# Attention with inducing points and a squared-ReLU layer: the opening of batch 0, with three score groups of batch 1 made beside it

## The chip, the cores and the metric

The kernel runs on one core of one Trainium2 chip. The metric is the device time of one execution in microseconds, the median of several runs. Batches, token groups and weight chunks are counted from 0, as in the code: batch 1 is the second batch.

## The reference

```python
# x: 4 x 12480 x 128, inducing: 32 x 128, w_in: 128 x 2048, w_out: 2048 x 128
def mab(q, kv):
    s = scale * (q @ kv.transpose(0, 2, 1))
    s = s - s.max(-1, keepdims=True)
    a = np.exp(s)
    a /= a.sum(-1, keepdims=True) + 1e-09
    return a @ kv
h = mab(I, x)                 # 32 points per batch, from all 12480 tokens
y = mab(x, h)                 # every token attends to its batch's 32 points
r = np.maximum(y @ w_in, 0.0)
out = (s * (r * r) + b) @ w_out
```

The weights arrive as float64; the rest is float32.

## The kernel before, in words

**The order of the work.** Every engine runs its own queue in order. The kernel builds these queues with a planner (`class Plan`): each piece of work is a generator that yields the engine, a length in microseconds and the events it waits for; the planner keeps a clock per engine and always issues the piece that its clock and the urgencies (`SQ`, `OUT`, `FIRST`, ...) prefer. So a changed length or urgency anywhere can reorder everything behind it. Loads are issued on SyncE's queue (SP) in the order of the table `ORDER`, later of the list `loads`; eight DMA semaphores are used in turn, so that a load is issued only when the eighth one before it has landed.

**Batch 0, first pass.** The 12480 tokens of a batch are 26 blocks of 480, in 7 groups of four blocks (group 6 has two). For batch 0 the groups x0 to x6 come as 13 halves of 480 KB (`load_first`, L420). For each group `p1_unit` makes the scores of the 32 points (L480), a maximum, an exponential, the transposed exponentials (L500) and the value products (L511) over tokens that must lie turned (tokens on partitions). Eleven halves are turned on TensorE (`turn_x`, L453, eight transposes each); group 5 is in `TURNED`, and its two halves come a second time, already turned, from a DRAM copy `xQ` (`load_turned`, L441, 120 partitions of 4 KB). Meanwhile `narrow` makes float32 of the float64 weight chunks (four of w_in, four of w_out, 512 KB each, L316) in seven steps on VectorE and ScalarE (L331 to L348), and `split_w_out` scales w_out by `s` and splits it into two float32r parts (L356, L358).

**From the last values to the first pair.** `h_unit` and `h_out` (L592, L609) combine the groups into the 32 points hT. `w_first` multiplies hT with each chunk of w_in (L632; the copies to `wst` on ScalarE, the residue on VectorE, L637): the points stand in for the tokens in the first layer. `attend_first` does the softmax of block 0 against the points (L843 to L870), turns it (L875) and copies it to `a2t` on ScalarE. Products that no one needs (`warm`, L1231) keep TensorE busy in the gaps.

**The main part.** For each block there are 8 pairs: two products a2t x wst (L928), a ReLU on ScalarE or VectorE (L942, L944), the square, rounded to float32r on ScalarE (L1010), the residue of the square on VectorE and GpSimd (L965, L987), and out products (L1035): two chunks times three parts, 64 products of 480 columns per block with the first two. The first `NATIVE` = 8 pairs (block 0) use two plain float32 products each instead, with the unsplit w_out. Beside the blocks of batch b run the attention of the same batch (L799) and, for batch b+1, scores (L701) and values (L742); some of them share a turn of TensorE (`visit`), with the tables `SCORES_WITH` and `VALUES_WITH` saying which group goes with which attention.

```python
# before.py, L86 on: batch 0 carries all seven score groups of batch 1
SCORES_WITH = (((6,), (0, 1), (2, 3), (4, 5), (), ()), ...
VALUES_WITH = (((), (), (), (), (0,), (2, 3)), ...
VALUES_AT = (((1, 20),), (), ())
```

Of the kernel before, what the change touches and what calls it, by code (L numbers as in the profile page):

```python
# [19 lines left out]
P = 128  # L20
T = 120
NQ = 4
# [14 lines left out]
SLIP = 0.1744  # L37
WEIGHT = 0.0178
LEAN = {'ACT': -0.5309, 'DVE': 0.6608}
R_LEAN = {'DVE': -0.2301, 'ACT': -0.2128}  # L40


M_U = -5.8018
R_U = 4.5067
SQ = 1.1237
MM = 0.2134
S_U = -0.7565
C_U = -10.6897
OUT_HI = 3.9914
OUT = 0.2122  # L50
FRONT = -1.1612
FIRST = -200.0
SPREAD = 74.0965
FIRST_FRONT = 0.3289
SPLIT_U = 237.6882

NATIVE = 8
H_U = -10.6844
N_U = -24.7788
W_IN_U = -167.7494  # L60
W_OUT_U = 10.3457
W_URGENCY = 3.9038
W_STEP = 19.8754
# [7 lines left out]
RUN = 512  # L71
A_OFF = 19
# [18 lines left out]
VISIT_U = -14.4858  # L91
# [3 lines left out]
class Plan:  # L95
# [7 lines left out]
    def __init__(self):  # L103
        self.free, self.events, self.units, self.end, self.start = {}, {}, [], 0.0, 0.0
        self.eng, self.by = None, {}
# [4 lines left out]
    def _step(self, unit, urgency, ready, src):  # L110
        want = next(unit, None)
        if want is not None:
# [9 lines left out]
            waits = [w for w in waits if not isinstance(w, float) and w != "both"]  # L122
            self.units.append([unit, urgency + more, (ready, src), engs, waits, urgency, lean, None, both])
# [26 lines left out]
    def run(self):  # L150
        while self.units:
            able = {}
            for u in self.units:
# [10 lines left out]
                able.setdefault(eng, []).append((at + WEIGHT * urgency, at, engs[eng], u))  # L164
# [7 lines left out]
            at, _, u, self.eng = min(picks, key=lambda x: x[0])  # L172
            self.units.remove(u)
            self.start, self.end = at, at + u[3][self.eng]
# [7 lines left out]
def tile_attn_relu2(ctx: ExitStack, tc: tile.TileContext, xT, xH, xN, xQ, indT, w_in, w_out, s_rep, b_rep, outT):  # L182
# [13 lines left out]
    const = ctx.enter_context(tc.tile_pool(name="const", bufs=1))  # L196
    xt_pool = ctx.enter_context(tc.tile_pool(name="xt", bufs=XT))
# [13 lines left out]
    def copy(out, in_):  # L211

        if plan.eng == "ACT":
            nc.scalar.copy(out=out, in_=in_)  # L214
        else:
            nc.vector.tensor_copy(out=out, in_=in_)

# [22 lines left out]

# [1064 lines left out]
```

## Time and profile before

| what | us |
|---|---|
| median of 3 runs | 1551.55 (1551.47 to 1551.56) |
| the profiled execution, its own time | 1552.4 |
| its span, first to last instruction | 1550.6 |
| TensorE busy | 1542.8 |
| VectorE, ScalarE, GpSimd busy | 1469.9, 1482.0, 1471.1 |
| first pair's products (L928) start | 46.36 |
| last out product ends, about | 1547 |

Busy time counts overlapping instructions of an engine once. The windows view gives it by stretch, the chain of waits names what each step waited for, and the timeline lists the instructions of an engine by start time; a merged row's length reaches to the end of its last instruction, so that neighbouring TensorE rows overlap, and the distance of two starts tells what a row really took.

### The profile page before, as it was taken

What the parts mean: (1) busy time and instruction counts of PE and PEld (TensorE: products, weight loads), DVE (VectorE), ACT (ScalarE), POOL (GpSimd) and SP (SyncE); (2) the same over time, 40 slices, a digit from 0 to 9 for tenths busy, and PEclk for the clock granted to TensorE, in tenths of its full rate; (3) what the DMA queues carried; (4) which work ended last, traced back from release to release, by engine and by line L of the source; (5) the groups of instructions that cost most, each with busy time, mean ns of one, the idle gap of its engine ahead of it and who ended that gap; (6) DMA issues with size and microseconds to landing.
All of it is one profiled execution on the core that took longest, in us unless ns stands there. A gap on an engine that the chain in (4) does not pass through costs nothing.

```text
span 1550.6 us, 24505 instructions
## 1 busy us (share of the span) xinstructions
PE 1542.8 (99%) x8135; PEld 1294.9 (84%) x8135; DVE 1469.9 (95%) x1648; ACT 1482.0 (96%) x1750; POOL 1471.1 (95%) x665
## 2 busy tenths in 40 slices
PE   9999999999999999999999999999999999999999
PEld 6688888888888888888888888888888888888887
DVE  5999999999999999999999999999999999999998
ACT  7899999999999999999999999999999999999998
POOL 0299999999999999999999999999999999999998
PEclk9999999999999999999999999999999999999999
DMA  8212321332233123123232321321313112112100
GB/s 300 64 56 80 122 72 71 114 130 96 68 111 115 39 103 115 39 103 115 71 85 80 118 76 66 115 80 65 112 60 96 32 52 71 40 44 71 57 22 32
DMA packets 53482, 130.12 MB, mean 84 GB/s; under 512 B 11262, under 2 KB 37758, under 8 KB 53358
## 3 DMA queue, kind: packets, MB, share of 16 engines
q1 hardware_dynamic: 53358, 128.56, 25.2%
q8 instruction: 66, 1.08, 0.3%
q14 instruction: 58, 0.48, 0.1%
HBM read 74.50 MB, written 25.56 MB: 65 GB/s over the span
## 4 chain that ended last, share of the span: by engine, by line
PE 96%; DMA 2%; DVE 1%; POOL 0%; issue 0%; ACT 0%; SPq 0%; ACTq 0%; DVEq 0%; POOLq 0%
PE x L1035 68%; PE h L928 23%; PE x L799 2%; PE h L742 1%; PE h L701 1%; DMA g<-in_w_in_dram 1%; DMA xn<-in_xQ_dram 1%; DMA s_sb<-in_s_rep_dram 0%; DVE g L965 0%; POOL g L987 0%; PE h L651 0%; ACT xn L214 0%; PE x L742 0%; PE x L511 0%; SPq L420 0%
## 5 line engine op out<-in xcount | busy, mean ns | idle before, releaser
L987 POOL TENSOR_TENSOR g<-g,g 128x960 fp32r<-128x960 f32 x657 | 1469.8, 2296 | 73.6 <-DVE g L965 67.8
L1035 PE MATMUL x<-g,w_hi 128*128 128x480 f32 x3296 | 1063.6, 375 | 0.0
L1010 ACT ACTIVATE g<-r 128x960 fp32r<-128x960 f32 (+1 forms) x805 | 796.2, 1029 | 16.5 <-DVE r L944 2.4
L965 DVE SCALAR_TENSOR_TENSOR g<-h,r 128x960 f32<-128x960 f32 x657 | 739.4, 1146 | 22.4 <-ACT r L942 14.2
L1035 PEld LDWEIGHTS x<-g,w_hi 128*128 128x128 f32 x3296 | 614.8, 187 | 91.8 <-POOL g L987 3.3
L942 ACT ACTIVATE r<-h 128x960 f32<-128x960 f32 x660 | 622.8, 969 | 27.3 <-PE h L928 26.3
L1035 PE MATMUL x<-g,w_lo 128*128 128x480 f32 x1648 | 617.3, 375 | 0.0
L928 PE MATMUL h<-a2t,wst 128*128 128x480 f32 x1664 | 484.7, 378 | 0.7 <-DVE g L965 0.7
L928 PEld LDWEIGHTS h<-a2t,wst 128*128 128x128 f32 x1664 | 306.6, 187 | 65.4 <-DVE x L805 7.3
L1035 PEld LDWEIGHTS x<-g,w_lo 128*128 128x128 f32 x1648 | 308.9, 187 | 42.8
L944 DVE TENSOR_SCALAR r<-h 128x960 f32<-128x960 f32 x172 | 197.7, 1150 | 9.5 <-PE h L928 7.1
L987 DVE TENSOR_TENSOR g<-h,g 128x960 fp32r<-128x960 f32 x167 | 192.6, 1154 | 12.7 <-ACT g L1010 1.3
L965 DVE SCALAR_TENSOR_TENSOR h<-h,r 128x960 f32<-128x960 f32 x167 | 193.1, 1157 | 6.4 <-ACT r L942 5.7
L1044 ACT ACTIVATE ob<-x,bias 128x480 f32<-128x480 f32 x103 | 68.0, 660 | 4.1 <-PE x L1035 3.9
L799 PE MATMUL x<-xt,hT 128*32 128x480 f32 x208 | 28.3, 578 | 0.0
L805 DVE STREAM_TRANSPOSE x<-x 128x480 f32<-128x480 f32 (+1 forms) x28 | 19.3, 688 | 2.2 <-PE x L799 2.1
L742 PEld LDWEIGHTS h<-xn,eT 128*32 128x32 f32 (+1 forms) x570 | 17.0, 109 | 5.0 <-issue 4.8
L823 DVE STREAM_TRANSPOSE x<-x 128x480 f32<-128x480 f32 (+1 forms) x28 | 19.5, 696 | 0.9
L742 PE MATMUL h<-xn,eT 128*32 128x128 f32 (+1 forms) x570 | 19.6, 273 | 0.0
L821 DVE TENSOR_TENSOR x<-x,l 128x480 f32<-128x480 f32 (+1 forms) x28 | 18.5, 661 | 0.7
L701 PE MATMUL h<-xt,ind_sb 128*32 128x480 f32 x156 | 19.1, 566 | 0.0
L810 DVE TENSOR_TENSOR x<-x,mx 128x480 f32<-128x480 f32 (+1 forms) x28 | 18.4, 656 | 0.1
(147 smaller groups left out, 375.4 us busy)
## 6 DMA issues: line engine op xcount, KB each, us to landing
xt<-in_xT_dram SPq DMA_DIRECT2D x41, 960.0 KB, 5.5
out_dram<-ob SPq DMA_DIRECT2D x104, 240.0 KB, 2.0
a2t<-hl SPq DMA_DIRECT2D x412, 60.0 KB, 2.0
xn<-in_xN_dram SPq DMA_DIRECT2D x18, 512.0 KB, 6.1
xn<-in_xN_dram SPq DMA_DIRECT2D x18, 448.0 KB, 6.7
r<-in_xH_dram SPq DMA_DIRECT2D x7, 480.0 KB, 8.2
xt<-in_xT_dram SPq DMA_DIRECT2D x7, 480.0 KB, 5.4
wst<-hl SPq DMA_DIRECT2D x48, 64.0 KB, 2.0
```

What stands on the lines that cost most here:

```text
L701: nc.tensor.matmul(ps[M * q:M * (q + 1), 0:BLK], ind_sb, xt[:, q], start=True, stop=True)
L742: nc.tensor.matmul(ps[M * c:M * (c + 1), 0:P], eT[0:rows, n], xn_tiles[b, g, half][0][0:rows, n - half * TH], start=m < P // M, stop=m + P ...
L799: nc.tensor.matmul(ps[M * q:M * (q + 1), 0:BLK], hT[:, 0:M], xt[:, q], start=True, stop=True)
L823: nc.vector.transpose(out=s, in_=s)
L928: nc.tensor.matmul(h[:, u, 0:BLK], wst[:, c * P:(c + 1) * P], A, start=True, stop=True)
L942: nc.scalar.activation(out=r, in_=hv, func=AF.Relu)
L944: nc.vector.tensor_scalar(out=r, in0=hv, scalar1=0.0, scalar2=None, op0=ALU.max)
L965: nc.vector.scalar_tensor_tensor(out=g, in0=hv, scalar=0.0, in1=r, op0=ALU.max, op1=ALU.mult)
L987: eng.tensor_tensor(out=g2, in0=g, in1=hi.bitcast(F32), op=ALU.subtract)
L1010: nc.scalar.activation(out=q["g1_t"][:, sl, :], in_=q["r_t"][:, sl, :], func=AF.Square)
L1035: nc.tensor.matmul(o, w, g, start=first and n == 0, stop=left == 0 and n == len(ops) - 1)
L1044: nc.scalar.activation(out=ob, in_=o, func=AF.Identity, bias=bias, scale=1.0 if scaled else s_sb)
```

## The change

Two groups come turned from DRAM instead of one: group 6 is added to `TURNED` (its one half is loaded to a buffer that an `hl` tile fills later, group 5's to the second `wst` buffer). So ten halves are turned on TensorE and three halves come turned. The scores of groups 6, 4 and 5 of batch 1 (`GAP`) are spawned with the opening: their loads stand in `ORDER` as ("n", ...), and they are no longer in the visits of batch 0, where value group 1 now goes with a visit instead of by itself. The raw w_out chunks and their split parts have buffers of their own (pool `w2`), where each pair of split tiles takes the place of two raw chunks. Of `narrow`, one step always runs on ScalarE or GpSimd, and in the chunks of `POOLED` another goes to GpSimd. The loads of `s` and `b` move from behind x1 to the end of `ORDER`. The planner's lengths are replaced; it gets an urgency per piece (`URGENT`) and a cost for changing between tiled and whole products (`SWITCH`).

```diff
-TURNED = (5,)
-ORDER = (
-    ("x", 0), ("x", 1), ("w_out", 0), ("x", 2), ("w_out", 1), ("x", 3), ("w_in", 0), ("x", 4), ("w_in", 1),
-    ("w_in", 2), ("x", 5), ("x", 6), ("w_out", 2), ("q", 5), ("w_in", 3), ("w_out", 3),
-)
-WARM = 6
+TURNED = (5, 6)
+X_HOME = (4, 1, 3, 0, 3, 2, 1)
+GAP = (6, 4, 5)
+ORDER = (('x', 0), ('w_in', 1), ('x', 1), ('x', 2), ('w_out', 2), ('w_out', 1), ('w_in', 0), ('w_out', 3), ('x', 3), ('x', 4), ('x', 5), ('x', 6), ('n', 6), ('q', 5), ('w_in', 2), ('q', 6), ('w_in', 3), ('n', 4), ('n', 5), ('w_out', 0), ('s', 0))
+SWITCH = 0.14
+POOLED = (('w_in', 2), ('w_out', 0), ('w_out', 2))
+GAP_U = 107.5895
+WARM = 7
...
-SCORES_WITH = (((6,), (0, 1), (2, 3), (4, 5), (), ()), ((0, 1), (2, 3), (4, 5), (), (), ()), ((0, 1), (2, 3), (4, 5), (), (), ()))
+SCORES_WITH = (((), (0, 1), (2, 3), (), (), ()), ((0, 1), (2, 3), (4, 5), (), (), ()), ((0, 1), (2, 3), (4, 5), (), (), ()))
...
-TOP_AT = (17, 11, 11)
-VALUES_WITH = (((), (), (), (), (0,), (2, 3)), ((), (), (), (0,), (1,), (2, 3)), ((), (), (), (0,), (1,), (2, 3)))
-VALUES_AT = (((1, 20),), (), ())
+TOP_AT = (11, 11, 11)
+VALUES_WITH = (((), (), (), (0,), (1,), (2, 3)), ((), (), (), (0,), (1,), (2, 3)), ((), (), (), (0,), (1,), (2, 3)))
+VALUES_AT = ((), (), ())
...
-        yield "ACT", 0.48
-        nc.scalar.activation(out=dst, in_=m, func=AF.Copy, scale=2.0**-20, bias=1.0)
+        yield dict(ACT=0.525, Pool=0.68), {"ACT": M_LEAN}, 0.0
+        if plan.eng == "ACT":
+            nc.scalar.activation(out=dst, in_=m, func=AF.Copy, scale=2.0**-20, bias=1.0)
+        else:
+            nc.gpsimd.tensor_scalar(out=dst, in0=m, scalar1=2.0**-20, scalar2=1.0, op0=ALU.mult, op1=ALU.add)
+        if name in POOLED:
+            yield "ACT", 0.525
+            nc.scalar.activation(out=m.bitcast(F32), in_=lo, func=AF.Copy, scale=2.0**-52)
+            yield "Pool", 1.37
+            nc.gpsimd.tensor_tensor(out=dst, in0=m.bitcast(F32), in1=dst, op=ALU.add)
+        else:
+            yield "DVE", 0.6, "both"
+            nc.vector.scalar_tensor_tensor(out=dst, in0=lo, scalar=2.0**-52, in1=dst, op0=ALU.mult, op1=ALU.add)
...
-        yield "DVE", 0.6, "both"
-        nc.vector.tensor_tensor(out=dst, in0=dst, in1=e.bitcast(F32), op=ALU.mult)
+        yield dict(DVE=0.6, Pool=1.37), 0.0, "both"
+        either().tensor_tensor(out=dst, in0=dst, in1=e.bitcast(F32), op=ALU.mult)
...
-        yield "ACT", 0.54, ("w_out", c)
-        nc.scalar.activation(out=w_hi[:, sl, :], in_=raw[:, sl, :], func=AF.Copy, scale=s_sb)
+        yield "ACT", 0.615, "s", ("w_out", c), *[("raw used", n) for n in mine], ("w2", half - 1)
+        if half not in w2:
+            w2[half] = [w2_pool.tile([P, 2 * WC // P, P], F32R, name="w2") for _ in range(2)]
+            plan.set(("w2", half))
...
+        nc.scalar.activation(out=w_hi, in_=raw[:, sl, :], func=AF.Copy, scale=s_sb)
...
+            elif what == "s":
+                yield "SP", 0.9
+                nc.sync.dma_start(out=s_sb, in_=s_rep)
+                nc.sync.dma_start(out=b_sb, in_=b_rep)
+                plan.events["s"] = landing(1.0)
+            elif what == "n":
+                yield from load_xt((), 1, n, 1)
+                i = GAP.index(n)
+                plan.spawn(
+                    scores(1, n, (lambda: bank[1], lambda: hs[0][:, 0])[i % 2],
+                           ("p1", 0, NG - 1), *([("scores", 1, GAP[i - 2])] if i > 1 else [])),
+                    FIRST + GAP_U + i + urgent("n", n),
+                )
```

Three places where instructions move. Line numbers of the second fence of each are the changed kernel's.

TensorE, from the attention of block 0 to its first five pairs. Before (L843 attention of block 0, L632 points times a chunk of w_in, L1231 products that nothing needs, L875 the turn into a2t, L928 pairs, L799 the next attention):

```order
L843 MATMUL x_85<-hT,xt 120x32 x4
L632 MATMUL h<-w_in_sb,hT 128x512 x2
L1231 MATMUL h<-g_115 128x480 x3
L1231 MATMUL h<-g_115 128x320 x2
L632 MATMUL h<-w_in_sb,hT 128x512
L1231 MATMUL h<-g_115 128x320
L875 MATMUL x_85<-accb,hl 128x120 x4
L632 MATMUL h<-w_in_sb,hT 128x512
L1231 MATMUL h<-g_115 128x320
L928 MATMUL h<-a2t,wst 128x480 x4
L799 MATMUL x_86<-xt,hT 32x480 x4
L928 MATMUL h<-a2t,wst 128x480 x6
```

and now (L972, L756, L1370, L1004, L1057, L928 in the same meaning; L830 the scores of batch 1):

```order
L972 MATMUL x_88<-hT,r 120x32 x4
L830 MATMUL h<-xt,ind_sb 32x480 x4
L756 MATMUL h<-w_in_sb,hT 128x512 x2
L830 MATMUL x_89<-xt,ind_sb 32x480 x2
L1004 MATMUL x_88<-accb,hl 128x120 x4
L1370 MATMUL h<-g_90 128x480 x2
L1057 MATMUL h<-a2t,wst 128x480 x2
L756 MATMUL h<-w_in_sb,hT 128x512 x2
L830 MATMUL x_89<-xt,ind_sb 32x480 x4
L1057 MATMUL h<-a2t,wst 128x480 x2
L928 MATMUL x_89<-r,hT 32x480 x4
L1057 MATMUL h<-a2t,wst 128x480 x6
```

Two of the three score groups stand ahead of the first pair, one behind it, and two of the four w_in products have moved behind it as well; over the whole opening 14 unneeded products before the first pair have become 9.

SyncE's loads, from the last halves of x. Before:

```order
L316 DMA g_301<-in_w_in_dram 128x1024
L420 DMA r<-in_xH_dram 128x960 x3
L316 DMA g_373<-in_w_out_dram 128x1024
L441 DMA xn<-in_xQ_dram 120x1024 x2
L316 DMA g_432<-in_w_in_dram 128x1024
L316 DMA g_441<-in_w_out_dram 128x1024
L892 DMA a2t<-hl 32x480 x8
```

and now:

```order
L535 DMA xt<-in_xH_dram 128x960 x3
L363 DMA xt<-in_xT_dram 128x960
L555 DMA wst<-in_xQ_dram 120x1024 x2
L393 DMA g_395<-in_w_in_dram 128x1024
L555 DMA hl<-in_xQ_dram 120x1024
L393 DMA g_409<-in_w_in_dram 128x1024
L363 DMA xt<-in_xT_dram 128x1920 x2
L393 DMA w_457<-in_w_out_dram 128x1024
L1346 DMA s_sb<-in_s_rep_dram 128x1
L1347 DMA b_sb<-in_b_rep_dram 128x1
```

A third turned half and a half of batch 1 have come in ahead of the last values' data; behind them stand two groups of batch 1, the last w_out chunk (chunk 0) and the loads of `s` and `b`.

VectorE, the softmax of block 0. Before (L850 to L870 are its steps, L348 a weight step, L637 the residue of a w_in product):

```order
L850 TENSOR_REDUCE mx_589<-x_85 120x4
L852 TENSOR_TENSOR x_85<-x_85,mx_589 120x128
L348 TENSOR_TENSOR w_in_sb<-w_in_sb,g 128x512
L856 TENSOR_REDUCE x_85<-x_85 120x4
L858 TENSOR_SCALAR x_85<-x_85 120x4
L861 RECIPROCAL l_599<-x_85 120x4
L637 TENSOR_TENSOR wst<-h,wst 64x512
L863 TENSOR_TENSOR x_85<-x_85,l_599 120x128
L637 TENSOR_TENSOR wst<-h,wst 64x512
L870 TENSOR_TENSOR hl<-x_85,hl 120x8x32
```

and now (L979 to L999 the steps, L429 a weight step, L833 the eviction of a score group):

```order
L979 TENSOR_REDUCE mx_598<-x_88 120x4
L981 TENSOR_TENSOR x_88<-x_88,mx_598 120x128
L429 SCALAR_TENSOR_TENSOR g<-g_409,g 128x512
L985 TENSOR_REDUCE x_88<-x_88 120x4
L987 TENSOR_SCALAR x_88<-x_88 120x4
L990 RECIPROCAL l_608<-x_88 120x4
L992 TENSOR_TENSOR x_88<-x_88,l_608 120x128
L833 TENSOR_SCALAR s,mx<-h 128x480
L999 TENSOR_TENSOR hl<-x_88,hl 120x8x32
```

Both residues have left this stretch, and one eviction has come in.

## Rows read from the trace of the kernel before

**Rows 1.** The page: span, and busy time, share, instructions of each engine.

```profile
span 1550.6 us, 24505 instructions
...
PE 1542.8 (99%) x8135; PEld 1294.9 (84%) x8135; DVE 1469.9 (95%) x1648; ACT 1482.0 (96%) x1750; POOL 1471.1 (95%) x665
```

**Rows 2.** Windows: stretch, length, busy (instructions) of PE, PEld, DVE, ACT, POOL; clock; DMA.

```profile
46.30:67.00 20.70, 20.70 (x100) 11.41 (x99) 20.33 (x29) 19.22 (x25) 0.76 (x1) 1.00 0.30 87
67.00:433.00 366.00, 366.00 (x1935) 307.77 (x1934) 348.52 (x394) 352.90 (x414) 363.64 (x163) 1.00 0.27 88
433.00:809.20 376.20, 376.20 (x1990) 320.01 (x1989) 362.10 (x405) 362.23 (x426) 373.64 (x168) 1.00 0.27 89
```

**Rows 3.** Waits of TensorE from 67 to 1551 us: total, times, longest.

```profile
PE h L928 <- DVE g L965: 0.7, 2, 0.4
```

**Rows 4.** Chain of waits, 20 to 48 us: start, length, what.

```profile
27.29 7.88 DMA xn<-in_xQ_dram
...
35.21 1.74 PE x L511 x44
...
37.51 0.64 PE h L609 x14
...
39.65 0.60 DVE w_in_sb L341
40.25 0.60 DVE g L343
...
41.39 0.59 DVE w_in_sb L348
...
42.65 0.70 DVE wst L637
...
43.70 0.69 DVE wst L637
...
44.91 0.54 PE x L875 x4
```

**Rows 5.** Timeline of TensorE: start, length to the last end, instruction.

```profile
15.32 1.09 PE L453 MATMUL h<-ident,r 128*120 128x128 f32 x8
...
40.57 1.96 PE L632 MATMUL h<-w_in_sb,hT 128*128 128x512 f32 x4
...
46.36 1.06 PE L928 MATMUL h<-a2t,wst 128*128 128x480 f32 x4
```

**Rows 6.** Windows of the opening, columns as in rows 2.

```profile
2.00:10.00 8.00, 7.94 (x46) 5.07 (x45) 1.29 (x5) 2.64 (x6) 0.00 (x0) 1.00 0.80 268
12.00:26.00 14.00, 13.77 (x186) 8.67 (x182) 10.21 (x23) 12.45 (x25) 0.00 (x0) 1.00 1.03 415
27.50:35.00 7.50, 6.36 (x74) 3.58 (x71) 6.17 (x16) 7.15 (x18) 0.00 (x0) 1.00 0.94 250
```

**Rows 7.** Windows of the scores of line L701 alone.

```profile
433.00:809.20 376.20, 6.36 (x52) 1.79 (x52) 1.00 0.27 89
```

**Rows 8.** Chain of waits, whole span: native and split out products.

```profile
52.38 3.25 PE x L1035 x8
...
1540.70 6.41 PE x L1035 x30
```

**Rows 9.** The page's groups: attention, values and scores on TensorE.

```profile
L799 PE MATMUL x<-xt,hT 128*32 128x480 f32 x208 | 28.3, 578 | 0.0
...
L742 PE MATMUL h<-xn,eT 128*32 128x128 f32 (+1 forms) x570 | 19.6, 273 | 0.0
...
L701 PE MATMUL h<-xt,ind_sb 128*32 128x480 f32 x156 | 19.1, 566 | 0.0
```

**Rows 10.** Timeline of VectorE and ScalarE, 36 to 48 us.

```profile
36.22 0.43 DVE L331 TENSOR_SCALAR g<-g 128x512 int32<-128x512 int32 x1 [1.06 <-DMA g<-in_w_in_dram]
...
45.48 0.56 ACT L214 CAST a2t<-x 128x480 fp32r<-128x480 f32 x1 [0.33 <-DVE wst L341]
...
47.03 0.97 ACT L942 ACTIVATE r<-h 128x960 f32<-128x960 f32 x1
```

More of the change, by code (lines that the diff above doesn't have):

```diff
@@ new lines @@
+URGENT = {
+    ('x', 3): -234.92,
+    ('w_in', 1): 384.17,
+    ('w', 1): 32.13,
+    ('n', 4): -165.82,
+    ('w', 0): -64.56,
+    ('turn', 4, 0): 27.09,
+    ('turn', 2, 1): 149.29,
+    ('x', 1): 14.97,
+    ('v', 6): 132.81,
+    ('turn', 2, 0): 24.44,
+    ('x', 6): 23.68,
+    ('x', 4): 29.01,
+    ('v', 5): 30.4,
+    ('turn', 0, 0): -1.93,
+    ('turn', 4, 1): 107.18,
+    ('x', 0): 28.8,
+    ('w_in', 3): -107.28,
+    ('w_in', 2): -33.54,
+    ('w_out', 0): 54.0,
+    ('e', 2): -73.1,
+    ('a',): -91.2,
+    ('split', 0): -52.36,
+    ('n', 2): -145.64,
+    ('n', 1): -53.73,
+    ('v', 1): 116.75,
+    ('turn', 6, 1): -158.08,
+    ('n', 6): 31.77,
+    ('turn', 3, 1): -58.68,
+    ('w_out', 1): 2.74,
+    ('w_in', 0): 6.86,
+    ('e', 4): -22.03,
+    ('turn', 1, 0): -1.74,
+    ('split', 1): -56.02,
+    ('turn', 5, 0): -28.41,
+    ('turn', 1, 1): 7.37,
+    ('w_out', 2): -4.46,
+    ('h',): -28.6,
+    ('v', 3): 7.59,
+    ('e', 6): -15.74,
+    ('turn', 5, 1): -19.49,
+    ('n', 3): 5.58,
+    ('split', 3): -0.2,
+    ('x', 2): 0.98,
+    ('n', 5): 1.62,
+    ('n', 0): 40.51,
+    ('turn', 3, 0): 31.87,
+    ('w_out', 3): -50.52,
+    ('e', 3): 27.69,
+    ('w', 3): 59.87,
+    ('w', 2): -21.65,
+    ('e', 5): -27.4,
+    ('e', 1): -29.11,
+    ('v', 4): 3.57,
+    ('e', 0): 0.92,
+}
@@ L121, in _step @@
             more = sum(w for w in waits if isinstance(w, float))
-            waits = [w for w in waits if not isinstance(w, float) and w != "both"]
-            self.units.append([unit, urgency + more, (ready, src), engs, waits, urgency, lean, None, both])
+            kind = True if "tiled" in waits else False if "whole" in waits else None
+            waits = [w for w in waits if not isinstance(w, float) and w not in ("both", "tiled", "whole")]
+            self.units.append([unit, urgency + more, (ready, src), engs, waits, urgency, lean, None, both, kind])
     def extend(self, us):
@@ L392, in homes @@
     def homes():
+        for _ in range(XT):
+            ring("xt", XT)
         for _ in range(2):
-            ring("xt", XT)
             ring("r", 2)
@@ L433, in x_used @@
         n = home["x", g]
[L434 to L435 removed]
+        if g == left["x"][n][-1] and g:
+            plan.set(("xt", n) if n < XT else ("r", n - XT))
     def load_turned(g):
@@ L446, in turn_x @@
         j = g * GR // SB + h
-        yield "PE", 0.99, *waits, ("x half", j), ("v done", j - 4)
+        n = turns.index(j)
+        if j:
+            yield "PE", 0.88, "whole", *waits, ("x half", j), *([("v done", turns[n - 4])] if n > 3 else [])
+        else:
+            yield "PE", 0.44, "whole", *waits, ("x part", 0, 0)
         xt = xt_tiles[0, g, 1][0].rearrange("p q (s t) -> p q s t", t=T)
-        t = home["xn"][j % 4]
+        t = home["xn", j].rearrange("p (a q c) -> p a q c", a=SB, q=NQ)
         ps = ps()
         for a in range(SB):
+            if a and not j:
+                yield "PE", 0.44, "whole", ("x half", j)
             for q in range(NQ):
@@ L683, in scores @@
         rows = M * nb
-        if b not in st:
+        if b not in begun:
+            begun.add(b)
+            yield "DVE", 0.15, *waits
             d = st[b] = {
@@ L1034, in out_part @@
         for n, (w, g) in enumerate(ops):
-            nc.tensor.matmul(o, w, g, start=first and n == 0, stop=left == 0 and n == len(ops) - 1)
+            nc.tensor.matmul(o, w(), g, start=first and n == 0, stop=left == 0 and n == len(ops) - 1)
         used()
@@ L1051, in out_part @@
         plan.set(("ob", blk_g))
+    turned_0 = wst_pool.tile([P, F], F32, name="wst")
+    turns = [j for j in range(NSB) if j * SB // GR not in TURNED]
     w_out_raw = wst_pool.tile([P, NF, P], F32, name="wst")
@@ L1130, in chain @@
                 for want in f(*args, ps):
-                    yield (*want, ("ob", blk_g - 1) if blk_g else "first") if first else want
+                    start = [("ob", blk_g - 1)] if blk_g else ["first", *[("scores", 1, g) for g in GAP[0::2]]]
+                    yield (*want, *start) if first else want
                     first = False
@@ L1191, in turn_work @@
         yield from turn_x(g, h, lambda: hs[turns.index(j) % 2], ("turn", before[turns.index(j)]))
-    turns = [j for j in range(NSB) if j * SB // GR not in TURNED]
     before = [-2, -1, *turns]
```

232 lines of the change are left out of this document (134 added, 98 removed).

## The prediction

> **What bounds the kernel now.** First the page: TensorE is busy for 1542.8 of the 1550.6 us of the span [rows 1], so nothing can move the time but TensorE's own work and the few microseconds in which it idles. Then the windows, by batch: from 67 us on TensorE is busy in the whole of each stretch, at a granted clock of 1.00 [rows 2], and in the waits of that time it stands idle in sight for 0.7 us in all [rows 3]. Thirty split products take 6.41 us, 0.214 us each [rows 8], and come back to back to the end. So the main part costs what its products cost. What else there is to win lies ahead of the first pair, at 46.36 us [rows 5].
>
> There the chain of waits tells what ends last, and it is not TensorE. From 27.29 to 35.17 us the chain is one piece: the two turned loads of group 5 [rows 4]. The windows say why: the DMA engines move 415 GB/s from 12 to 26 us, and 250 from 27.5 to 35, while they are busy all the time [rows 6]. Only then come the last value products (35.21), the 32 points (h_out, 37.51), steps of VectorE, the turn into `a2t` (44.91) and the first pair [rows 4, 5]. Between h_out and that turn VectorE is the bound, and other work stands in the chain there: weight steps (0.60, 0.60, 0.59) and two residues of the points' layer (0.70, 0.69) [rows 4].
>
> **The change, part by part.** The profiled execution took 1552.4 us, its span 1550.6; the median of the runs is 0.85 below the first. I make the sum as a difference within the profile and add it to the median.
>
> *A. The last turned load lands later.* Two loads come in ahead of it: half a group of batch 1 (480 KB) and a third turned half. At 415 GB/s 480 KB take 1.18 us [rows 6]. A turned half is dearer: the 7.5 us window at 250 GB/s moved 1.88 MB, of which 0.98 MB were the two turned halves; the other 0.90 MB at 415 GB/s take 2.15 us, which leaves 5.35 us, 2.7 for each [rows 6]. The low bound is an ordinary half's 1.18, the high one half of the chain's row, 7.88 / 2 = 3.94 [rows 4]. I take 2.7, as it is worked out from the bytes moved. Something is won back: the loads of `s` and `b`, 128 rows of one number each, leave the start. The window from 2 to 10 us moved 268 GB/s [rows 6]; at 415 it would have moved (415 - 268) x 8 us = 1.18 MB more, 2.8 us of transfer. The trace does not tell how much of that is theirs and how much the start itself; between 0 and 2.8 I take 1.3, near the middle. So the landing is at 35.17 + 1.18 + 2.7 - 1.3 = 37.75 us, with bounds 35.17 + 1.18 + 1.18 - 2.8 = 34.7 and 35.17 + 1.18 + 3.94 = 40.3.
>
> The Trainium skill says in "DMA: Bandwidth & Descriptors", section "Why a DMA increments its semaphore by 16 and not by 1", that a transfer spreads over the largest number of engines up to 16 that divides its partitions. For 120 that is 15, and by that rule alone an estimate for a turned half is 16/15 of 1.18, 1.26 us; the sum would be 1.4 us lower, near 1550.9. The 250 GB/s of the row stand against it, so I keep to the row.
>
> *B. From the landing to h_out.* Before, the values after the landing take 1.74 us (44 records, half of them weight loads, so 22 products), and h_out starts 0.56 us after their end [rows 4]. Now the last load feeds 8 products: 8 / 22 x 1.74 = 0.63. So h_out starts at 37.75 + 0.04 + 0.63 + 0.56 = 38.98, which is **+1.47** against 37.51.
>
> *C. From h_out to the first pair.* Both residues leave VectorE's softmax stretch (0.70 + 0.69), one weight step goes out ahead of the maximum, of whose 0.60 some 0.4 stood in the way, as attend_first starts only at 39.65; an eviction of a score group comes in. Its nearest row is a residue of about its size, 0.69 [rows 4]. -0.70 - 0.69 - 0.4 + 0.69 = **-1.1**; bounds -1.6 (the eviction falls in a gap) and -0.3 (the steps moved out were hidden by the exponential). So the first pair starts at 46.36 + 1.47 - 1.1 = 46.7.
>
> *D. Work that now stands behind the first pair.* Two of the four w_in products of 512 columns, and score group 5, come after it, where TensorE is busy 20.70 of 20.70 us [rows 2] and so pays for all of it. Two such products take less than 1.96 us, a merged length that reaches over the next product's start, and 0.90 each by their pitch in the row [rows 5]: 1.8 with bounds 1.6 and 1.96. A score group is 8 records of the 52 that take 6.36 us in a batch [rows 7], 0.98. Together **+2.8**.
>
> *E. The main part loses three score groups.* They are 20 of these 52 records: 20 / 52 x 6.36 = **-2.45** us [rows 7], all of it on the packed engine.
>
> *F. What costs nothing.* One turn of a half (eight transposes, 15.32 us, 1.09 [rows 5]) goes; TensorE had no part in the chain while it waited for the turned loads, so that is worth 0 as long as the load lands last. The same holds for the two score groups ahead of the first pair: they take the place of products that nothing needs (1.51 us at 41.97 among others) [rows 4, 5]. The weight steps moved to ScalarE and GpSimd and the own homes of w_out make VectorE's queue shorter, away from the chain. ScalarE gets two scale copies of w_out straight behind the copy into `a2t` (45.48) and ahead of its first ReLU (47.03) [rows 10]; they wait for `s`, now the last load. Between the landing at 37.75 and `s` stand 2944 KB of other loads, 7.3 us at 415 GB/s [rows 6], so `s` lands after 45.1, about when the copy into `a2t` begins; ScalarE's first ReLU may move by a microsecond or two. TensorE has D's 2.8 us of work meanwhile, so I take 0. The rest of the new order: TensorE runs packed before, so 0, with 1.5 either way.
>
> The sum: +1.47 - 1.1 + 2.8 - 2.45 = **+0.7**, or **1552.3 us**. With the bounds of A and of the order taken together this case's own range is 1550.2 to 1554.4: no change that a measurement of this kernel could tell, for which I take 0.2%, some 3.1 us.
>
> **The rivals.** *R1, the opening ends with TensorE, not with the load.* If the turned halves run at an ordinary pace, and the start regains its 2.8 us, the landing is at 34.7. Then h_out comes when TensorE gets there: 37.51 less the 1.07 it now waits for the loads and less the turn's 1.02, 35.4, or -2.1. With C, D and E: -2.1 - 1.1 + 2.8 - 2.45 = -2.85, **1548.7**. For it speaks that the rate of 250 may belong to other traffic of those 7.5 us; against it, that the slow window begins just where the turned loads do.
>
> *R2, the new order takes out small gaps in the main part.* From 46.3 to 1546.9 are 1500.6 us; 6,624 split products at 6.41 / 30 are 1415.3, the native ones cost about 10 more, attention 28.3, values 19.6, scores 19.1 [rows 8, 9]. Some 8 us are left, of which the points' and layers' products of three batches take about half. With 3 of the remaining 4 gone: **1549.3**. Against it: only 0.7 us of waiting is to be seen [rows 3].
>
> *R3, slower: the loads behind each other.* If a turned half costs the chain's 3.94 us and nothing is won at the start, the landing is at 40.3, +2.55. Then every load behind it moves too: w_out chunk 0 ends the 2944 KB behind it, 7.3 us, at 47.6; its seven narrowing steps took from 36.22 to the 41.98 of the last in the chain for a w_in chunk, 5.8 us [rows 4, 10], and the first native out product needs it (52.38 [rows 8]). It and the scale copies that hold ScalarE's queue until `s` is there add about 0.5: **1555.5**. This decides from a landing after about 39.7. For it: the chain's own row; against it: the bytes that the windows count.
>
> That the change does not do what it says is in the forecast already: the score groups were to fill time of products that nothing needs, yet one of three groups and two w_in products fall behind the first pair, so 2.8 of work take the place of 2.45.
>
> **How the numbers follow.** Forecast 0.56, R1 0.16, R2 0.12, R3 0.16. Faster by over 0.2% is below 1548.45: half of R1 and of R2, and little of the forecast, 0.19. Slower by over 0.2% is above 1554.65: R3 and a little of the forecast, 0.17. Within: 0.64. The range takes in the centres of all three rivals, 1548.3 to 1555.6.
>
> **What would show it.** Right: the last turned load lands at about 37.8 us, TensorE waits for it, h_out at 39.0, first pair at 46.7; between the first and second pair two w_in products and 8 score records; 32 instead of 52 score records of batch 1 behind it; busy to the last product at clock 1.00. R1 would show no wait for a turned load; R3 a landing near 40, and idle time of TensorE between 46 and 60 us with w_out chunk 0 or `s` as the releaser; R2 an opening as long as forecast and a shorter batch 1 or 2. The forecast is wrong if the first pair starts before 45 or after 49, or if batches 1 to 3 change in length by more than 1.5 us.

## The result, and the profile after

The changed kernel takes **1566.79 us** (median of 4 runs, 1565.68 to 1568.77) against 1551.55 (4 runs): ratio 1.0098, interval 1.0086 to 1.0111. It is slower by 15.2 us, where the forecast was 1552.3 and the range ended at 1555.6. The runs of the kernel before lie within 0.2 us of each other, those of the changed one are 3 us apart; its longest, 1568.77, has a mean granted clock of 0.997, the other three 1.000. The profiled execution took 1565.85 us, 13.45 more than the profiled one of before.

The page's first rows, span and busy times, to be held against [rows 1]:

```profile
span 1564.1 us, 24449 instructions
...
PE 1550.7 (99%) x8123; PEld 1300.2 (83%) x8123; DVE 1478.4 (95%) x1651; ACT 1476.3 (94%) x1738; POOL 1475.0 (94%) x675
```

TensorE has 12 instructions fewer and is busy for 7.9 us more. Where the time lies is told by the windows of the changed kernel, in the columns of [rows 2] (its first pair starts at 47.19, its first block ends at about 72.8 us):

```profile
46.90:72.50 25.60, 24.05 (x110) 12.14 (x110) 23.10 (x35) 21.57 (x28) 2.31 (x3) 1.00 0.23 68
72.50:438.80 366.30, 365.67 (x1914) 309.36 (x1914) 350.76 (x390) 352.78 (x412) 360.62 (x162) 1.00 0.25 82
438.80:818.10 379.30, 379.30 (x1990) 321.02 (x1989) 365.77 (x407) 360.86 (x422) 372.91 (x168) 1.00 0.26 88
```

Two things stand out. The first is the opening. ScalarE's eviction of the first block, before and now:

```profile
66.88 0.75 ACT L1044 ACTIVATE ob<-x,bias,s_sb 128x480 f32<-128x480 f32 x1
```

```profile
72.80 0.74 ACT L1173 ACTIVATE ob<-x,bias,s_sb 128x480 f32<-128x480 f32 x1
```

It starts 5.9 us later: so much the opening lost, and TensorE is idle for 1.55 us of the first row's stretch, where it was busy throughout in [rows 2]. The second is the main part. Batch 1, whose tables were not changed, has the same 1990 TensorE instructions as in [rows 2], the same clock, TensorE busy throughout, and takes 379.30 us instead of 376.20. Waits explain none of it; this is every wait of TensorE from 67 us on (compare [rows 3]):

```profile
PE x L1164 <- DVE hl L959: 0.9, 2, 0.5
```

So the products themselves had become longer. The last entry of the chain of waits is a run of split out products, in the changed kernel 40 of them:

```profile
1551.72 8.68 PE x L1164 x40
```

8.68 / 40 is 0.217 us, against 0.214 in [rows 8]. The starts of the instructions in the trace say it sharper (the pitch is the distance of two neighbouring starts; products followed after 217 to 222 ns are called 219s from here on): from 90 us on, 1,706 of some 4,890 out products are 219s, and the rest are nearly all followed after 213 to 215 ns; in the kernel before 22 are. Those at 219 are mostly every second product of a pair of two, they come in stretches of up to 90 us, and then the pitch is the ordinary one for some time. 1,706 at some 5.2 ns are 8.9 us, and the others are half a nanosecond longer too. That is two thirds of the 13.45 us, and nothing in the prediction had to do with it.

### The profile page after: what moved, and what is told of

Read it like the earlier page. It is cut to its first block, busy times and chain, and to the rows that moved or that the text cites. A ratio compares the mean times of both kernels' runs of the same rounds, so it can differ in the third digit from the quotient of the medians.

```text
span 1564.1 us, 24449 instructions
## 1 busy us (share of the span) xinstructions
PE 1550.7 (99%) x8123; PEld 1300.2 (83%) x8123; DVE 1478.4 (95%) x1651; ACT 1476.3 (94%) x1738; POOL 1475.0 (94%) x675
## 4 chain that ended last, share of the span: by engine, by line
PE 94%; DVE 2%; ACT 2%; DMA 1%; issue 1%; SPq 0%; POOL 0%; DVEq 0%; ACTq 0%; POOLq 0%
PE x L1164 67%; PE h L1057 22%; PE x L928 2%; PE h L871 1%; PE h L830 1%; DVE g L1094 1%; DMA hl<-in_xQ_dram 1%; ACT g L1139 1%; ACT r L1071 0%; DMA g<-in_w_in_dram 0%; DVE h L1094 0%; PE x L633 0%; PE h L573 0%; DVE r L1073 0%; PE h L775 0%
## 5 line engine op out<-in xcount | busy, mean ns | idle before, releaser
L1164 PE MATMUL x<-g,w 128*128 128x480 f32 x4944 | 1190.8, 377 | 1.0 <-DVE hl L959 0.9
L1164 PEld LDWEIGHTS x<-g,w 128*128 128x128 f32 x4944 | 927.7, 188 | 140.5 <-DVE hl L959 1.9
L1057 PE MATMUL h<-a2t,wst 128*128 128x480 f32 x1664 | 486.6, 379 | 0.1
L1057 PEld LDWEIGHTS h<-a2t,wst 128*128 128x128 f32 x1664 | 309.1, 188 | 63.7 <-issue 7.6
L1073 DVE TENSOR_SCALAR r<-h 128x960 f32<-128x960 f32 x176 | 202.4, 1150 | 15.9 <-PE h L1057 13.4
L928 PE MATMUL x<-xt,hT 128*32 128x480 f32 x200 | 27.3, 578 | 0.0
L943 DVE TENSOR_REDUCE x<-x 128x15 f32<-128x480 f32 (+1 forms) x28 | 18.4, 657 | 1.4 <-ACT x L941 1.1
L937 DVE TENSOR_REDUCE mx<-x 128x15 f32<-128x480 f32 (+1 forms) x28 | 18.1, 645 | 0.4
```

The costliest lines, as they stand in the source:

```text
L928: nc.tensor.matmul(ps[M * q:M * (q + 1), 0:BLK], hT[:, 0:M], xt[:, q], start=True, stop=True)
L1057: nc.tensor.matmul(h[:, u, 0:BLK], wst[:, c * P:(c + 1) * P], A, start=True, stop=True)
L1073: nc.vector.tensor_scalar(out=r, in0=hv, scalar1=0.0, scalar2=None, op0=ALU.max)
L1164: nc.tensor.matmul(o, w(), g, start=first and n == 0, stop=left == 0 and n == len(ops) - 1)
```

## The experiments

**The address of the weights.** In the kernel before, the split weights of w_out begin at byte 9024 of a partition, which is 320 within 512. Their own pool puts them at 10240, a multiple of 512. One product's weights take 512 bytes of a partition, so all of them begin at the same place within 512. The moving rows of the out products (the squares and their residues) begin at 460 within 512 in both. In the changed kernel alone the place was put back; in the kernel before alone it was moved, to three places; the order of every engine stays, and of the other tiles only five small constants, which no out product reads, change their place.

```diff
# a_w9024: the tiles of the split weights ahead of five small constants, not behind them
+    const2 = ctx.enter_context(tc.tile_pool(name="const2", bufs=1))
-    bias = const.tile([P, 1], F32, name="bias")
+    bias = const2.tile([P, 1], F32, name="bias")
...
# b_w10240: the same move in the kernel before, the other way round (the five lines are taken out further down)
+    bias = const.tile([P, 1], F32, name="bias")
+    ident = const.tile([P, P], F32, name="ident")
+    ones = const.tile([P, M], F32, name="ones")
+    rebias = const.tile([P, 1], F32, name="rebias")
+    sel = const.tile([P, P], F32, name="sel")
     w_hi = const.tile([P, NF, P], F32R, name="w_hi")
     w_lo = const.tile([P, NF, P], F32R, name="w_lo")
```

> The changed kernel with nothing but an address changed: the split w_out tiles begin at byte 9024 of a partition, where they begin in the kernel before, instead of 10240. Theory A (the address of the weights makes the second of two out products take 219 ns instead of 213): the 219s go, 1752 of them from 90 us on in the profile at 5.5 ns, 9.6 us, so 1557 us, and the runs agree within 0.3 us. Theory B (it is the new order of the work, or that the weights lie in four tiles): it stays at 1566 to 1568 us with as many 219s.

> The kernel before with nothing but an address changed: w_hi and w_lo begin at byte 10240 instead of 9024, where the changed kernel has them; order and instructions as before. Theory A (address): second out products at 219 ns in stretches, 1558 to 1563 us, runs that differ by 1 us and more. Theory B (order or four tiles): 1551.5 us, no 219s.

> The kernel before with the split weights 64 bytes higher, at 9088: a multiple of 128 but not of 512. Theory A, if a multiple of 128 is what hurts: 1558 to 1563 us; if it takes a multiple of 512: 1551.5. Theory B: 1551.5.

> The kernel before with the split weights at 9216, a multiple of 512 (and 1024) as 10240 is. Theory A: 1558 to 1563 us, if the place within 512 bytes is what matters; 1551.5 if it is 10240 itself or a larger period. Theory B: 1551.5.

Measured: a_w9024 1558.63 us (ratio to before 1.0042, 1.0027 to 1.0056), b_w10240 1561.68 (1.0061, 1.0044 to 1.0078), b_w9088 1551.70 (0.9999, 0.9989 to 1.0010), b_w9216 1563.13 (1.0070, 1.0050 to 1.0090). The chain's last run of out products in b_w10240 and in a_w9024:

```profile
1549.65 6.51 PE x L1035 x30
```

```profile
1545.39 8.55 PE x L1165 x40
```

The reader is to hold 6.51 against the 6.41 of [rows 8] (the same 30 products), and 8.55 against 8.68 above (the same 40). Theory A holds in both directions: 8.2 us of the 15.2 go with the address (1566.79 to 1558.63), and the kernel before loses 10 to 11 us with nothing but that move. Neither the new order nor the four tiles are needed for it. What is left to explain is 6.9 us.

The 8.2 is less than the address cost the main part. From the first block's eviction to the last one's the profile of the changed kernel takes 1487.6 us and that of a_w9024 1478.0, so 9.6 us; but the opening of a_w9024's profiled execution is 3.2 us longer (its first block's eviction starts at 75.98). There the last turned load lands at 39.59 us, not 37.65, TensorE is busy for only 2.5 of the 6 us from 34 to 40, and then its granted clock falls to half, 1.2 GHz, while it is busy throughout (windows, columns as in [rows 2]):

```profile
38.00:40.00 2.00, 0.66 (x8) 0.60 (x10) 1.60 (x8) 1.82 (x6) 0.62 (x1) 0.99 1.02 392
40.00:42.00 2.00, 2.00 (x28) 1.97 (x24) 1.43 (x3) 0.59 (x3) 1.27 (x1) 0.50 1.02 420
```

From the last landing to the first pair it takes 10.74 us there and 9.54 in the changed kernel's profile, where the clock stays at 1.00. The profile of a_g19 (below), with its weights at 10240, has such a stretch at half clock too, so it does not come with the address.

A second set asked which of the two places counts. It moves the rows by 64 bytes, or puts the weights at 448:

```diff
-G_OFF = 3
+G_OFF = 19
```

> The changed kernel as it is, split weights at 10240, with only the squares (the moving operand of the out products) 64 bytes further in their tiles. Theory G (it is the distance of the moving rows from the weights within 512 bytes): from 52 bytes it becomes -12, and the share of 219s changes, to none or to more. Theory H (it is the weights' own place, a multiple of 512): the 219s stay, 1566 to 1568 us.

> The kernel before with the split weights at 9152, which is 448 within 512, 12 bytes ahead of the moving rows (460 within 512). Theory G (the distance decides): it is the same distance of 12 as in a_g19 and the 219s are as many as there, some 2900, 1566 us or more. Theory H (a multiple of 512 is what hurts): none, 1551.5.

> The kernel before with only the squares (the moving operand) 64 bytes further in their tiles, 12 instead of 460 within 512; the split weights stay at 9024, 320 within 512. Theory G (the rows' distance behind the weights decides, small ones are bad): it is 204 bytes now, none of the 219s, 1551.5 us. Theory J (the rows' place alone is bad at 12, as in a_g19): 219s, 1560 us and more.

Measured: a_g19 1575.04 us (ratio 1.0149, 1.0131 to 1.0168), b_w9152 1558.14 (1.0036, 1.0023 to 1.0049), b_g19 1561.15 (1.0065, 1.0042 to 1.0088). All nine kernels together, the places counted within 512 bytes, the 219s from 90 us on (the first two products of a pair, a2t x wst, called up here, are named where more than 60 of them have that pitch too):

```
kernel      weights  rows   out products at 219    time us
before        320    460          22               1551.55
a_w9024       320    460          26               1558.63
b_w9088       384    460          33               1551.70
b_w9152       448    460         869  (+371 up)    1558.14
changed         0    460        1706               1566.79
b_w10240        0    460        1882               1561.68
b_w9216         0    460        1931               1563.13
b_g19         320     12        1659  (+235 up)    1561.15
a_g19           0     12        2928               1575.04
```

Both places matter. Theory H (only a multiple of 512) falls with b_w9152 and b_g19, theory G (only the distance) with b_w9152, whose distance of 12 is that of a_g19 with a third of the 219s, and its form that small distances are bad with b_g19 as well, at a distance of 204; theory J (only the rows' place) with b_w10240. What rule joins the two is left open. The Trainium skill says in "SBUF — State Buffer", section "Who interferes with whom", that TensorE reads its moving operand and its weights through two independent ports, and that only the port pair of VectorE and GpSimd is contended for. By that alone one would have expected these moves to cost nothing; the runs of the kernel before show 6 to 11 us for four of the five moves, and the measurement decides.

**The opening, with the tables of the change.** On a_w9024, so that the 219s don't blur them, four parts of the change were undone by its own tables: a weight step back from GpSimd, one score group back to the main part, one turned group less, `s` and `b` early.

```diff
# a_pool_w0
-POOLED = (('w_in', 2), ('w_out', 0), ('w_out', 2))
+POOLED = (('w_in', 2), ('w_out', 2))
# a_gap2 (ORDER, SCORES_WITH and VALUES_WITH of batch 0 with it)
-GAP = (6, 4, 5)
+GAP = (6, 4)
# a_turned1 (and no ('q', 6) in ORDER)
-TURNED = (5, 6)
+TURNED = (5,)
# a_s_early
-ORDER = (('x', 0), ('w_in', 1), ('x', 1), ('x', 2), ...
+ORDER = (('x', 0), ('w_in', 1), ('x', 1), ('s', 0), ('x', 2), ...
```

> The changed kernel with the split weights at 9024, and the narrowing step of w_out chunk 0 that the change gave to GpSimd back on VectorE; TensorE's order up to the second pair stays. In the changed kernel VectorE's step that makes the low part of w_out took 1.74 us instead of 0.70 while GpSimd's 1.28 us step ran, an eviction stood behind it, and TensorE waited 1.2 us for that. Theory C (the two engines hinder each other): the step is back near 0.7 to 0.8 us, TensorE's wait goes, and the first native out product comes some 1 us nearer to the first pair: about 1557.5 us against 1558.6. Theory D (that step is long for another reason): it stays at 1.7 us and the time at 1558.6.

> The changed kernel with the split weights at 9024 and only two score groups in the opening; group 5 goes back into a visit of batch 0 (with the value groups of batch 0 as in the kernel before). Its 8 records leave the stretch between the first and second pair (0.98 us) and return in the main part (0.98 us). If the loss of the opening is TensorE's work and waits behind the first pair: from the first pair to the first native out product 8.2 us become 6 or less, and the whole is 1.2 us faster, 1557.4. If it is the late landing: no change of the whole, 1558.6.

> The changed kernel with the split weights at 9024 and group 6 turned on TensorE again, so that two turned halves are loaded instead of three. If the turned loads set the end of the opening, as the prediction has it: the last of them lands 2 to 3 us earlier, the 32 points and the first pair come 2 us earlier, the whole is 1556 to 1557 us. If the opening ends with something else by now: first pair at 47 us and later, 1558 to 1559.5, with the turn of one half more (1.1 us) on TensorE.

> The changed kernel with the split weights at 9024 and the loads of s and b back behind x1, as before the change. If they cost the start what the prediction took, 1.3 us of loading (bounds 0 and 2.8), the last turned load lands that much later and the whole is 1558.6 + 1.3 less what the scale copies gain from having s early. If they cost nothing there, it is 1558 us or a little less.

Measured: a_pool_w0 1571.55 us (ratio 1.0126, 1.0111 to 1.0141), a_gap2 1569.68 (1.0114, 1.0097 to 1.0131), a_turned1 1557.46 (1.0038, 1.0023 to 1.0053), a_s_early 1571.73 (1.0131, 1.0116 to 1.0146). Three of the four missed what every theory expected by 10 us or more. The planner had made another order of the whole kernel out of each edit. TensorE's longest waits from 67 us on in a_pool_w0:

```profile
PE h L1058 <- DVE g L1095: 3.6, 9, 0.8
PE x L1165 <- DVE hl L960: 1.2, 3, 0.5
PE x L1165 <- POOL g L1117: 0.9, 1, 0.9
PE x L1165 <- ACT g L1140: 0.3, 2, 0.2
```

a_w9024 waits there for 0.9 us in all. So the whole times of a_pool_w0, a_gap2 and a_s_early say nothing about the opening, and these three are inconclusive as asked. One reading of a_pool_w0 stands on its own: the instructions of VectorE's line that makes the low parts of w_out, first in a_w9024, then in a_pool_w0 (shortest, median, longest ns):

```profile
L460 DVE SCALAR_TENSOR_TENSOR w<-wst,s_sb,w x4: 743/745/1745, 53.7 to 69.6; 128x512 fp32r<-128x512 f32 x4
```

```profile
L460 DVE SCALAR_TENSOR_TENSOR w<-wst,s_sb,w x4: 722/747/751, 56.0 to 66.5; 128x512 fp32r<-128x512 f32 x4
```

Without GpSimd's step beside it the long one is gone. a_turned1 kept a sound main part and came out between its two expectations. Its last turned load landed at 34.08 us instead of 39.59. Its first pair starts later (51.78 against 50.33), because the planner has put the next attention, a score group and all the w_in products ahead of it; the first native out product starts 2.8 us earlier (55.81 against 58.57), after a wait of 1.20 us for a w_out chunk that VectorE narrows. So 5.5 us at the load gave 2.8 there, and the opening had another end by then, VectorE's queue.

**The opening, with the order held.** The next edits are made where an instruction is issued, and the planner doesn't see them, so that the order of everything else stays. The first pads the turned copy to 128 partitions.

```diff
# a_q128 and, but for the names of the tiles, b_q128
-        "xQ": np.ascontiguousarray(x[0].reshape(...).transpose(...).reshape(-1, T, SB * NQ * C)),
+    xq = np.zeros((N // (SB * BLK), P, SB * NQ * C), x.dtype)
+    xq[:, :T] = x[0].reshape(...).transpose(...).reshape(-1, T, SB * NQ * C)
...
-            nc.sync.dma_start(out=home["xn", j], in_=xQ[j])
+            nc.sync.dma_start(out=home["q", j], in_=xQ[j])
# a_s_pin, in opening(), behind the loads of x1
+                if n == 1:
+                    nc.sync.dma_start(out=s_sb, in_=s_rep)
+                    nc.sync.dma_start(out=b_sb, in_=b_rep)
```

> The kernel before with nothing changed but the turned copy: its rows are padded from 120 to 128 with zeros, so a turned half is loaded to 128 partitions; the 8 rows more are read by nothing. Theory E (a turned load is slow, 2.7 us against 1.2, because of its 120 partitions): the two halves take 1.3 us each, the last lands some 2.7 us earlier, and the kernel gains the 1.07 us that TensorE waited for them, 1550.5 against 1551.5. Theory F (it is slow for another reason: the array in DRAM, or where it is written): they take 2.7 us as before and the time stays.

> The changed kernel with the split weights at 9024 and the same padding to 128 partitions; the order of every engine is the same. Theory E: three halves at 1.3 instead of 2.7 us, the last lands 3 to 4 us earlier and the first pair starts 2 us earlier or more: about 1556 us against 1558.6. Theory F: 1558.6.

> The changed kernel with the split weights at 9024 and the loads of s and b issued behind x1 as in the kernel before, everything else in the order that the changed kernel has (the planner does not see the move). By the prediction's term the start loses 1.3 us of loading (bounds 0 and 2.8) and the last turned half lands that much later, 1559.9 us less what the scale copies gain; if the loads of s and b are free where they stood, 1558.6.

Measured: b_q128 1550.51 us (11 runs, 1550.25 to 1551.56; ratio 0.9994, 0.9985 to 1.0002), a_q128 1553.87 (1.0014, 1.0005 to 1.0023), a_s_pin 1559.54 (1.0049, 1.0035 to 1.0062). The windows over the turned loads, of the changed kernel and of a_q128 (columns as in [rows 6]):

```profile
27.00:37.00 10.00, 7.46 (x133) 5.39 (x125) 5.97 (x18) 6.34 (x15) 0.59 (x1) 1.00 1.02 273
```

```profile
28.00:34.50 6.50, 5.55 (x91) 4.18 (x91) 4.47 (x12) 5.19 (x13) 0.00 (x0) 1.00 1.03 420
```

420 GB/s instead of 273: each turned half lands 1.3 us behind the load ahead of it in a_q128, and 2.0 to 2.2 behind it in the changed kernel. Theory E holds as far as the edit goes: it fills the 128 partitions and with that changes the array in DRAM too, and no run parts the two. The padding is worth 4.8 us to the changed kernel with its weights at 9024 and 0.9 to the one before. In the profiles the last landing is 4.9 us earlier than in a_w9024 (34.69 against 39.59) and the first pair 5.7 (44.61 against 50.33); the other 0.8 lies behind the landing, where the clock now stays at 1.00. b_q128 is the fastest kernel of this study, 16 us below the change; against the kernel before its interval reaches just past no difference. a_s_pin differs from a_w9024 by less than their executions differ among themselves, and in its profile the last turned load landed 0.8 us earlier (38.76), not later; the 1.3 us of that term stay unsettled.

**From the first pair to the first native out product.** In a_q128 the first pair starts at 44.61 us, in b_q128 at 44.45; the first native out product at 52.84 and 47.84. The kernel before has the same distance as b_q128, 3.39 us from its first pair (46.36 [rows 5]) to this line of its timeline:

```profile
49.75 1.77 PE L1035 MATMUL x<-g,wst 128*128 128x480 f32 x4
```

In a_q128 it is 8.23. So 4.8 us were lost here, where the prediction had 2.8. The timeline of the changed kernel, TensorE, then VectorE and GpSimd:

```profile
47.19 0.70 PE L1057 MATMUL h<-a2t,wst 128*128 128x480 f32 x2
48.08 2.25 PE L756 MATMUL h<-w_in_sb,hT 128*128 128x512 f32 x4 [0.20 <-DVE w_in_sb L434]
50.26 1.01 PE L830 MATMUL x<-xt,ind_sb 128*32 128x480 f32 x8
51.20 0.70 PE L1057 MATMUL h<-a2t,wst 128*128 128x480 f32 x2
53.08 1.01 PE L928 MATMUL x<-r,hT 128*32 128x480 f32 x8 [1.18 <-DVE s L833]
54.02 1.56 PE L1057 MATMUL h<-a2t,wst 128*128 128x480 f32 x6
55.41 1.80 PE L1164 MATMUL x<-g,wst 128*128 128x480 f32 x4
```

```profile
50.59 1.74 DVE L459 SCALAR_TENSOR_TENSOR w<-wst,s_sb,w 128x512 fp32r<-128x512 f32 x1
52.35 0.66 DVE L833 TENSOR_SCALAR_CACHE_REDUCE s<-x 128x480 f32<-128x480 f32 x1
```

```profile
50.49 1.28 POOL L423 TENSOR_TENSOR wst<-g,wst 128x512 f32<-128x512 f32 x1 [1.42 <-ACT g L421]
```

TensorE's attention (53.08) waits for the eviction of score group 5 (52.35), which stands behind the low part of w_out (50.59). That step takes 1.74 us; GpSimd's ends at 51.77, and 0.56 us later VectorE's ends. So VectorE seems to do most of its step only when GpSimd is done. The Trainium skill says in "SBUF — State Buffer", section "Who interferes with whom", that a VectorE instruction with two inputs in SBUF contends with a GpSimd instruction that reads SBUF. The trace agrees: this step reads two tiles, and the other three of its line, with GpSimd idle, take 0.74 to 0.75 us. a_defer, on a_q128, issues that one step later:

```diff
-        nc.vector.scalar_tensor_tensor(out=w_lo, in0=raw[:, sl, :], scalar=s_sb, in1=w_hi.bitcast(F32), ...)
+        late.append(lambda: nc.vector.scalar_tensor_tensor(out=w_lo, in0=raw[:, sl, :], scalar=s_sb, ...))
+        if len(w2) > 1:
+            while late:
+                late.pop(0)()
```

> The kernel a_q128 (changed, weights at 9024, padded loads) with one instruction later in VectorE's queue: the first step that makes a low part of w_out, which took 1.73 us beside a GpSimd step of 1.30 and before an eviction that TensorE waited for, is issued with the next ones of its kind, some 15 us later. Theory C (VectorE stood still until GpSimd was done, and TensorE behind it): the step takes 0.75 there, TensorE's wait of 1.2 us goes, the stretch from the first pair to the first native out product falls from 8.2 to 6.9 us, and the whole from 1553.9 to 1552.5. Theory D (that stretch has another bound, such as ScalarE's or VectorE's length): 1553.9.

Measured: 1552.61 us (10 runs, 1552.22 to 1553.00; ratio 1.0001, 0.9992 to 1.0010). TensorE in a_defer:

```profile
48.92 0.70 PE L1065 MATMUL h<-a2t,wst 128*128 128x480 f32 x2
49.78 1.01 PE L936 MATMUL x<-r,hT 128*32 128x480 f32 x8 [0.16 <-DVE s L841]
50.72 1.55 PE L1065 MATMUL h<-a2t,wst 128*128 128x480 f32 x6
52.11 1.81 PE L1172 MATMUL x<-g,wst 128*128 128x480 f32 x4
```

The wait fell from 1.17 to 0.16 us, the stretch from 8.2 to 7.2 (44.90 to 52.11), the whole by 1.26 (1553.87 to 1552.61). That the step's place cost this is shown; how much of it is the wait for GpSimd and how much the step's own 0.75 us the run does not part. With these three faults out (the address, the narrow loads, this step's place), the change is level with the kernel before, but not with the padded one: b_q128 is 1 to 2 us faster.

**The residues alone.** b_res is b_q128 with the residues of the points' layer issued behind the last step of VectorE's softmax, where the change has the first of them.

```diff
-        nc.vector.tensor_sub(out=lo, in0=ps[P // 2:P], in1=lo.bitcast(F32))
+        late.append(lambda: nc.vector.tensor_sub(out=lo, in0=ps[P // 2:P], in1=lo.bitcast(F32)))
+        if soft:
+            late.pop(0)()
```

> The kernel b_q128 (before, with padded loads) and the two residues of the points' layer taken out of VectorE's softmax stretch to behind its last step, which is the part of the change that the prediction gave -0.7 - 0.69 us. If VectorE bounds that stretch: the turn starts 1.0 to 1.4 us after h_out earlier than in b_q128 and the whole is 1549.3. If ScalarE's cast ahead of the last step or the weights' residues then bound the first pair: 1550.0 to 1550.5.

Measured: 1552.01 us (ratio 0.9995, 0.9987 to 1.0004), a miss: nothing gained; each set against the kernel before that ran beside it, b_res and b_q128 are level (0.9995 and 0.9994). VectorE's last softmax step and the residues, and TensorE, in b_res:

```profile
42.47 0.42 DVE L874 TENSOR_TENSOR hl<-x,hl 120x256 fp32r<-120x256 f32 x1 [0.51 <-ACT hl L214]
43.38 1.30 DVE L639 TENSOR_TENSOR wst<-h,wst 64x512 fp32r<-64x512 f32 x2 [0.48 <-PE h L634]
```

```profile
43.32 0.46 PE L882 MATMUL x<-accb,hl 120*128 120x120 f32 x4
44.73 1.12 PE L634 MATMUL h<-w_in_sb,hT 128*128 128x512 f32 x2 [0.95 <-DVE wst L639]
```

The turn comes earlier relative to h_out (6.8 us after it, 7.4 in b_q128), less than the 1.4 us taken out, as the last step now waits for ScalarE's cast. And the residues, late now, hold TensorE's next w_in product for 0.95 us, ahead of the first pair, which starts 9.6 us after h_out (8.8 in b_q128). The work had not been in the way so much as one of several things that end there together.

## Why the prediction was wrong

Between the two profiled executions the 13.45 us add up as follows: the landing and h_out +1.1, from h_out to the first pair -0.3, from there to the first native out product +4.8, from there to the first block's eviction +0.3, the main part +7.4, the end +0.2. The main part is E's -2.3 and the 9.6 us of the address. So two steps failed: F, which put the new homes of w_out at nothing, and D, which counted products and no waits.

**Bounds: right as far as read.** TensorE is packed at a granted clock of 1.00 after as before. That "the main part costs what its products cost" held; that a product costs 0.214 us was taken for fixed, and this is where it broke.

**F failed, the largest step.** "What costs nothing" counted the own homes of w_out as something that makes VectorE's queue shorter. They are a change of address as well, and that put a third of the out products at 219 ns: 8.2 us by a_w9024 on the whole, 9.6 of the main part, and 10.0 and 11.4 in the kernel before by a move to such a place. "TensorE runs packed before, so 0, with 1.5 either way" had bounds for the order and none for the length of a product. No rival had this mechanism.

**A: right.** The last turned load landed at 27.44 + 10.20 = 37.64 us (forecast 37.75). The chain of the changed kernel, the counterpart of the entry in [rows 4]:

```profile
27.44 10.20 DMA hl<-in_xQ_dram
...
37.78 0.96 PE x L633 x14
```

That it came so near was partly luck. The turned halves landed 2.0 to 2.2 us behind the load ahead of them, not 2.7 (2.0 and 3.1 in the kernel before, 1.7 to 2.4 in a_w9024), the half group of batch 1 took 2.3 instead of 1.18, and the start-up gain is not settled. In other executions the landing was at 39.59 (a_w9024) and 38.76 us (a_s_pin), inside the bounds. The cause of the dear loads, left open there, goes away with the padding to 128 partitions. By the rule of the Trainium skill ("DMA: Bandwidth & Descriptors", section "Why a DMA increments its semaphore by 16 and not by 1") the prediction's estimate was 1.26 us a half. The trace does not bear that size out: 2.0 to 2.2 were measured at 120 partitions, 1.3 at 128, far more than that ratio.

**B: nearly.** h_out started at 38.61 us (forecast 38.98), 0.97 us after the landing; two of its 14 products slipped in before the last values, at 38.48.

**C: mis-sized.** From h_out to the first pair it was 8.58 us (38.61 to 47.19) against 8.85 before: -0.3 instead of -1.1, at the end of its bounds. The 0.94 us of scores that F had as free in that stretch stand ahead of the w_in product whose cast holds ScalarE's queue, and the cast for VectorE's last softmax step is behind that; in b_res taking the residues out alone, to where they hold a w_in product, gained nothing.

**D: mis-sized.** 2.8 us were the products alone. Measured from the first pair to the first native out product: 8.22 us against 3.39, so 4.8. The score group took 0.94 us (forecast 0.98), the two w_in products 2.2 (forecast 1.8); what D left out is that TensorE also waits there for VectorE, 1.2 us behind one step (a_defer: 1.26 on the whole) and 0.2 for narrowed weights.

**E: right.** From the first block's eviction to the last block's the a_w9024 profile takes 1478.0 us, that of before 1480.3: -2.3 for -2.45.

**The rivals.** R3 had the side right and the reason wrong: w_out chunk 0 and `s` landed at 44.84 and 45.08 us (forecast for `s` after 45.1) and TensorE waited for neither. R1's condition, turned loads at an ordinary pace, was made true in a_q128; it gave 1553.9, not 1548.7, as R1 had D's 2.8 for 4.8, C's -1.1 for -0.4, and h_out at 35.4 for 36.2. R2's small gaps did not go; its count of 6,624 split products is 16 too high (64 in each of 103 blocks and block 0's 16 up products make 6,608), so that 3.4 us more were left than it says.

## What to carry to other kernels

When a tile that TensorE reads moves, compare the distance of two product starts, not the waits: 5 ns more on a third of the products cost more than every wait here. Here padding a load from 120 to 128 partitions was worth more than the bytes it added: try it before counting bytes. Undo parts of a planned kernel where instructions are issued, not in the planner's tables, or each test measures another schedule.

## What was not expected of the hardware

- The place of the weights and of the moving rows within 512 bytes decides whether a product's pitch is 213 to 214 ns throughout or also 219, in stretches that come and go (the table above).
- In a full queue loads of 480 KB to 120 partitions landed 2.0 to 2.2 us behind the load ahead of them in the changed kernel (1.7 to 3.1 in the others read), the same rows padded to 512 KB and 128 partitions 1.2 to 1.5.
- A 512-column step of VectorE with two inputs in SBUF took 1.74 instead of 0.75 us beside a GpSimd step of 1.28.
- In a_w9024's opening TensorE, busy for 2.5 of the 6 us from 34 to 40, was then granted 0.50 of its clock, in the middle of the chain to the first pair; with the padded loads (a_q128) the clock stayed at 1.00.
